# Attention and GEGLU block: the range flag's branch moved ahead of the last work, and a re-timed plan for the first chunks and the DMA transposes

## Chip, cores, metric

One core of one Trainium2 chip (eight cores; the others are unused). The metric is device time in microseconds of one execution, as the median of several runs. Engine names: PE is the matmul engine (TensorE), PEld its weight loads, ACT the scalar engine, DVE the vector engine, POOL GpSimd, SP the engine that issues most DMAs.

## What is computed

A pre-layernorm transformer block on 2048 tokens of width 512, bf16 inputs and output, with 32 heads of width 16 and an FFN width of 1792:

```python
x = A_x
h = x + attention(layernorm(x)) @ wo     # qkv = layernorm(x) @ wqkv; softmax(q k^T / 4) v, 32 heads
h2 = h + (gelu(n @ w_gate) * (n @ w_up)) @ w_down   # n = layernorm(h), tanh form of gelu
```

Most of the work is the softmax: 32 heads of 2048 x 2048 scores. A tile of the kernel is 128 keys by 512 query columns of one head (or of several heads with fewer queries each), so there are 2048 tiles, each of which needs 65,536 exponentials.

## The kernel before

**A fast program and a fallback.** `fast_path` computes the softmax without subtracting a row maximum. At its end `check` (L2031) compares all row sums with a safe range, reduces the comparison over partitions with one PE matmul and casts the sum to an integer `flag`, which is 128 if every row is in range. `max_path` is a second, complete program with a row maximum. In `emit` (L1183) each engine runs its fast instructions, waits until the flag is written, loads it into a register and branches: with 128 it jumps over its instructions of the fallback, otherwise it waits for the whole fast program and runs them. SP then waits for the final count of every DMA semaphore (L1194).

**A planned order.** The fast program is written as many generators ("streams") that yield operations with an engine, a planned duration, and the buffers that they read and write. The scheduler `Sched` (L889) plays them against each other: of the operations that are ready it takes the one that can start first, ties going to the stream with the lower priority number, to which a small random part (seed in L906) is added. What comes out is a fixed list per engine, with semaphore waits where a buffer is shared; the chip runs each list in order. So planned durations and priorities act only through the order. A planned DMA takes SP 0.5 us and lands after a time made of its size, a queue shared by all, and 0.8 us (L999 to L1003). `TTAB` is the planned time of an activation-table load; `PT` is a ring of 16 tiles, so ACT can be at most 16 tiles ahead of the products that consume them.

**Start.** `loads` (L1338) brings x in pieces (tiles 0 and 1, tiles 2 and 3, then four tiles at a time) and the weights, all on SP. For each tile of 128 tokens `ln1` (L1383) takes mean and variance on DVE, `ln1_rstd` (L1412) adds epsilon and raises to the power -0.5 on POOL, `ln1_norm` (L1420) normalizes, on DVE for tiles 0 to 7 and with three small-to-large POOL instructions for the others, and `ln1_T` (L1440) transposes: on PE with an evacuation by ACT (tiles 0 to 2) or DVE (3 to 7), by DMA for tiles 8 to 15. `first` (L1471) projects the keys and queries of the first 512 tokens; `proj_kq` and `proj_v` project the rest. `ones_v` (L1368) writes the ones beside V that make the row sums, with four POOL memsets once the first exponential is planned. Chunk 1 means tokens 512 to 1023 here (tiles 4 to 7); its streams have priority 9 (2 + 7c), the first chunk's -7 and below.

**Middle.** Score matmuls (L1582, recorded at L1329, the helper for matmuls in a part of the array) go to PSUM; ACT exponentiates two tiles in one instruction (L1335) into `PT`. A share of the tiles is exponentiated by DVE and POOL with integer arithmetic instead (`dget`, `dconv` L1706, `dchain` L1719 to L1726), from the 20th projection on. The products with V accumulate per unit; `ofin` (L1806) turns the result with a DMA transpose (OAT), divides, and per chunk of queries `leave` turns the heads' outputs (OT), `post` projects, adds x, normalizes and turns again (hT). Query chunks have 512, 512, 256, 256, 256, 128, 128 tokens. The FFN of a chunk (`gates`, `ups`, `downs`, L1943 to L2024) runs on PE beside the scores of later chunks. `fill` (L2054) puts dummy matmuls (L2052) where PE would idle.

**End.** After the last exponential only FFN work is left. `downs` (L2005) forms the down product of 128 tokens in one PSUM bank with 14 matmuls of 512 columns; `down_evac` (L2018) adds h on DVE and stores from SP. `check` has priority base_dl + 60, behind gates and ups (+30) and downs (+40).

## Time and profile before

| what | us |
|---|---|
| median of 5 runs | 818.82 (818.29 to 821.78) |
| the profiled execution | 820.27 |
| its span in the trace | 818.5 |
| PE busy | 793.9 (97%) |
| DVE busy | 759.2 (93%) |
| ACT busy | 766.7 (94%) |
| POOL busy | 251.9 (31%) |
| ACT exponentials (L1335), 776 of them | 722.4, mean 1.08 |
| DVE first step of its own tiles (L1706), 496 | 325.7, mean 0.68 |
| DMA transposes: OAT 31, OnT 15, hnT 15, xnT 8 | 2.3 to 2.4 from issue to landing (medians) |

The span is the time between the first and the last record of the profiled execution; the run's own time is 1.7 longer. Busy time of PE is modelled for overlapping matmuls, so a full PE need not be at its peak. A wait line names the waiting engine and line, then who released it, the total, the number and the longest. A timeline line has start, duration, engine, line, operation, output and input, count, and in brackets the idle time before it and who ended it. In the view by windows each engine's busy time in a stretch stands with its number of instructions, then the granted PE clock (1.00 is full). Register loads, branches and semaphore waits are not in these views, but the trace has records of them.

### The profile page before, as it was taken

Reading aid. Unit: us, or ns where it says so; the run is one execution under the profiler, and the core shown is the slowest. Engines: PE = TensorE matmul, PEld = TensorE weight load, DVE = VectorE, ACT = ScalarE, POOL = GpSimd, SP = SyncE. Lnnn points to the kernel's source line nnn. Section 1 sums busy time; section 2 is a strip of 40 time slices with the busy share of each in tenths; the row PEclk is TensorE's granted clock in tenths of the full one; section 3 lists DMA queues with packets and bytes.
Section 4 is the critical chain, followed back from the end, with each engine's and each line's share of the span. In section 5 each row is a group of like instructions: output and inputs, shape, how many; then the busy total and the mean of one; then the engine's idle time right before and its main releaser. Section 6 shows DMA issues by size and latency. Waiting matters only on the chain.

```text
span 818.5 us, 20339 instructions
## 1 busy us (share of the span) xinstructions
PE 793.9 (97%) x8325; PEld 277.9 (34%) x8325; DVE 759.2 (93%) x1238; ACT 766.7 (94%) x809; POOL 251.9 (31%) x305
## 2 busy tenths in 40 slices
PE   8999999999999999999999999999999999999997
PEld 3322222222222222222233333333343344444555
DVE  7569999999999999999989998999999999999974
ACT  4699999999999999999999999999999999999961
POOL 5714355423343221222243222223232231342220
PEclk9899999999999999999999999999999999999999
DMA  6200000700020000010021001000010200110000
GB/s 206 52 8 1 7 8 7 276 21 8 19 47 15 14 8 1 14 34 14 6 46 30 20 9 23 18 22 27 8 20 15 40 8 8 28 29 16 16 22 18
DMA packets 49878, 24.33 MB, mean 30 GB/s; under 512 B 39280, under 2 KB 48752, under 8 KB 49776
## 3 DMA queue, kind: packets, MB, share of 16 engines
q1 hardware_dynamic: 49776, 22.95, 11.0%
q8 instruction: 67, 1.10, 0.6%
q14 instruction: 35, 0.29, 0.1%
HBM read 11.80 MB, written 2.10 MB: 17 GB/s over the span
## 4 chain that ended last, share of the span: by engine, by line
PE 45%; DVE 31%; ACT 13%; issue 6%; DMA 3%; POOL 1%; SPq 0%; DVEq 0%; ACTq 0%; POOLq 0%
PE pbank L1329 27%; PE pbank L1328 16%; DVE dXE L1706 14%; ACT PT L1335 11%; DVE dXE L1721 6%; DVE dXE L1719 4%; DVE dXE L1726 4%; PE pbank L2052 1%; DVE GUT L1972 1%; DMA OAT<-OA 1%; ACT GUT L1985 1%; DMA wqkv_sb<-in_A_wqkv_dram 1%; DVE OA L1810 1%; POOL dXE L1723 1%; ACT L1335 1%
## 5 line engine op out<-in xcount | busy, mean ns | idle before, releaser
L1335 ACT ACTIVATE PT<-pbank 128x1024 bf16<-128x1024 f32 x776 | 722.4, 1082 | 17.5 <-PE pbank L1329 14.9
L1329 PE MATMUL pbank<-QT,KT 32*128 32x512 bf16 (+1 forms) x2304 | 346.4, 360 | 11.6 <-ACT PT L1335 3.6
L1706 DVE TENSOR_SCALAR dXE<-pbank 128x512 uint16<-128x512 f32 x496 | 325.7, 682 | 11.1 <-PE pbank L1329 9.7
L1723 POOL TENSOR_TENSOR dXE<-dXE 128x512 f16<-128x512 f16 x124 | 157.3, 1269 | 375.2 <-DVE dXE L1721 375.2
L1329 PEld LDWEIGHTS pbank<-QT,KT 32*128 32x128 bf16 x2304 | 89.2, 91 | 290.8 <-ACT PT L1335 201.1
L1329 PE MATMUL pbank<-PT,VA 128*32 128x256 bf16 (+2 forms) x2708 | 130.7, 293 | 0.0
L1721 DVE TENSOR_TENSOR dXE<-dXE 128x1536 f16<-128x1536 f16 x124 | 123.9, 1000 | 0.9
L1719 DVE TENSOR_SCALAR dXE<-dXE 128x2048 uint16<-128x2048 uint16 x124 | 92.4, 745 | 0.1
L1726 DVE TENSOR_SCALAR dXE<-dXE 128x2048 uint16<-128x2048 uint16 x124 | 87.9, 713 | 4.8 <-POOL dXE L1723 3.5
L1329 PE MATMUL pbank<-dXE,VA 128*32 128x256 f16 (+2 forms) x1752 | 76.6, 290 | 0.7 <-DVE dXE L1726 0.5
L1328 PE MATMUL pbank<-hnT_c,wg_sb 128*128 128x256 bf16 (+2 forms) x392 | 70.0, 291 | 0.3 <-issue 0.3
L1329 PEld LDWEIGHTS pbank<-PT,VA 128*32 128x32 bf16 x2708 | 48.2, 96 | 61.5 <-issue 58.6
L2052 PE MATMUL pbank<-ones_bf,zero_bf 128*128 128x512 bf16 x203 | 68.6, 388 | 0.0
L1328 PE MATMUL pbank<-hnT_c,wu_sb 128*128 128x256 bf16 (+2 forms) x392 | 59.3, 289 | 3.0 <-DVE GUT L2000 3.0
L1328 PE MATMUL pbank<-wd_sb,GUT 128*128 128x512 bf16 x224 | 60.1, 382 | 0.0
L1832 POOL TENSOR_TENSOR Otok<-OAT,LINV 128x128 bf16<-128x128 bf16 (+2 forms) x52 | 28.6, 564 | 82.6 <-DVE LINV L1826 82.5
L1329 PEld LDWEIGHTS pbank<-dXE,VA 128*32 128x32 bf16 x1752 | 30.9, 96 | 30.6 <-issue 17.4
L2000 DVE TENSOR_TENSOR GUT<-pbank,GUT 128x512 bf16<-128x512 f32 (+1 forms) x57 | 36.7, 673 | 2.5 <-ACT GUT L1985 1.5
L1328 PE MATMUL pbank<-xnT,wqkv_sb 128*128 128x512 bf16 (+1 forms) x152 | 38.4, 349 | 0.0
L1328 PEld LDWEIGHTS pbank<-hnT_c,wu_sb 128*128 128x128 bf16 x392 | 29.5, 98 | 25.0 <-issue 10.7
L1972 DVE CAST GUT<-pbank 128x512 bf16<-128x512 f32 (+1 forms) x53 | 35.6, 673 | 1.0 <-PE pbank L1328 0.7
L1328 PEld LDWEIGHTS pbank<-hnT_c,wg_sb 128*128 128x128 bf16 x392 | 24.7, 97 | 29.6 <-issue 27.1
(80 smaller groups left out, 348.6 us busy)
## 6 DMA issues: line engine op xcount, KB each, us to landing
xres<-in_A_x_dram SPq DMA_DIRECT2D x16, 128.0 KB, 2.3
out_dram<-out_sb SPq DMA_DIRECT2D x16, 128.0 KB, 1.7
wg_sb<-in_B_w_gate_dram SPq DMA_DIRECT2D x1, 1792.0 KB, 7.4
wu_sb<-in_B_w_up_dram SPq DMA_DIRECT2D x1, 1792.0 KB, 11.3
wd_sb<-in_B_w_down_dram SPq DMA_DIRECT2D x1, 1792.0 KB, 15.4
x_sb<-in_A_x_dram SPq DMA_DIRECT2D x3, 512.0 KB, 8.6
wqkv_sb<-in_A_wqkv_dram SPq DMA_DIRECT2D x1, 896.0 KB, 7.9
x_sb<-in_A_x_dram SPq DMA_DIRECT2D x2, 256.0 KB, 3.0
```

Of the source, the lines that this page charges most:

```text
L1328: return lambda e: e.matmul(o, l, r, start=start, stop=stop)
L1329: return lambda e: e.matmul(o, l, r, start=start, stop=stop, tile_position=tile)
L1335: return lambda e: e.activation(out=o, in_=i, func=func, **kw)
L1706: yield Op("dve", 0.603, lambda e: e.tensor_scalar(out=dXE[G["k"] % NX][:, 0, j, :], in0=pbank[:, b, :], scalar1=XMIN + 1024.0 * CENTER, s ...
L1719: yield Op("dve", 0.07 + 0.133 * n, lambda e: e.tensor_scalar(out=W, in0=X, scalar1=0x3ff, scalar2=0xb800, op0=ALU.bitwise_and, op1=ALU.bi ...
L1721: yield Op("dve", 0.066 + 0.267 * nd, lambda e: e.tensor_tensor(out=W[:, 0:nd, :].bitcast(F16), in0=W[:, 0:nd, :].bitcast(F16), in1=X[:, 0 ...
L1723: yield Op("pool", TPOOL, lambda e, j=j: e.tensor_tensor(out=W[:, j, :].bitcast(F16), in0=W[:, j, :].bitcast(F16), in1=X[:, j, :].bitcast( ...
L1726: yield Op("dve", 0.07 + 0.133 * (h1 - h0), lambda e, h0=h0, h1=h1: e.tensor_scalar(out=X[:, h0:h1, :], in0=X[:, h0:h1, :], scalar1=0x7c00 ...
L1832: yield Op("pool" if turned else "dve", 0.15 + 0.55 / len(slots) if turned else 0.06 + 0.28 / len(slots), lambda e, o4=o4, lx=lx, o_ap=o_a ...
L1972: yield Op("dve", 0.07 + 0.001042 * n * CHUNKS[c], lambda e: e.tensor_copy(out=o_ap, in_=i_ap), reads=[("pb", b)], writes=keys, extra=dE)
L2000: yield Op("dve", 0.07 + 0.001042 * n * CHUNKS[c], lambda e: e.tensor_tensor(out=o_ap, in0=u_ap, in1=o_ap, op=ALU.mult), reads=[("pb", b)] ...
L2052: return Op("pe", TMM, lambda e: e.matmul(pbank[:, b, :], zero_bf[:], ones_bf[:], start=False, stop=False, skip_group_check=True), reads=[ ...
```

## The change

- **Branch.** `Plan.run` can run a part of an engine's list. For ACT the list is cut in front of the last evacuations, for SP at the place where `check` has been planned; there the engine waits for the flag and branches. The rest of its list then stands in an `Else` (and, for the fallback, at the head of the `If`). PE, DVE and POOL branch at the end as before. SP's final waits are sorted by when the semaphore was last used.
- **Last token tile.** `last_down` makes two halves of 256 columns, in each of which an identity matmul puts h into PSUM first; `last_evac` copies each half out on ACT and stores it, one half from SP, the other from ACT.
- **Check.** Its priority becomes base_dl + 20.
- **DMA transposes.** SP is planned busy for 1.25 us, and the landing later by 2.0 us (OAT, OT, hT) or 0.6 (xT).
- **Start.** The ones are written by one DVE memset at priority -9; the memset of a PSUM bank comes ahead of the masks. Chunk 1's streams have priority -4 or -3.5, its key projection -5. Epsilon is added on DVE for tiles 4 to 7 too; DVE normalizes tiles 8 and 9 as well; POOL's two small factors become one instruction; ACT evacuates tiles 4 and 5. Planned load sizes differ.
- **Planner.** TTAB 1.3 becomes 1.45, the seed 9 becomes 66.

```diff
@@ Plan.dma
         self.dma_count[semkey] += 16
+        self.dma_last[semkey] = sum(self.dma_count.values())
...
-    def run(self, name, h):
+    def run(self, name, h, lo=0, hi=None):
         e = self.eng[name]
-        for (fn, waits, sig, dsem) in e.ops:
+        for (fn, waits, sig, dsem) in e.ops[lo:hi]:
...
@@ Sched
-        self.rng = random.Random(9)
+        self.rng = random.Random(66)
...
             self.done[tok] = self.pipe + 0.8
+            if op.dma[0] in TURNS:
+                self.t[op.eng] = start + 1.25
+                self.done[tok] += TURNS[op.dma[0]]
...
-TTAB = 1.3
+TTAB = 1.45
+TURNS = dict(OAT=2.0, OT=2.0, hT=2.0, xT=0.6)
...
@@ emit
-            P.run(name, h)
+            cut = P.cut.get(name, len(P.eng[name].ops))
+            P.run(name, h, 0, cut)
             h.wait_ge(P.sems["dve"], P.flag_count)
             r = h.alloc_register("flag_" + name)
             h.reg_load(r, flag[0:1, 0:1])
             with h.If_ne(r, 128):
+                P.run(name, h, cut)
                 for sem, v in fin:
                     if v:
                         h.wait_ge(sem, v)
                 FP.run(name, h)
+            if cut < len(P.eng[name].ops):
+                with h.Else():
+                    P.run(name, h, cut)
             if name == "sp":
-                for k, v in P.dma_count.items():
-                    h.wait_ge(P.sems[k], v)
+                for k in sorted(P.dma_count, key=lambda k: P.dma_last[k]):
+                    h.wait_ge(P.sems[k], P.dma_count[k])
...
@@ ones_v
-        for q in range(4):
-            yield Op("pool", 0.6, lambda e, q=q: e.memset(VA[:, 4 * q:4 * q + 4, :, 16:17], 1.0), writes=["VA_ones"], gate=lambda: C["exp"] >= 1, port=True)
-        yield Op("pool", 0.1, lambda e: e.memset(VF[:, NVA:NVA + 15], 0.0), writes=["VA_ones"])
+        yield Op("dve", 0.62, lambda e: e.memset(VA[:, :, :, 16:17], 1.0), writes=["VA_ones"])
+        yield Op("dve", 0.1, lambda e: e.memset(VF[:, NVA:NVA + 15], 0.0), writes=["VA_ones"])
...
@@ ln1, ln1_rstd, ln1_norm, ln1_T
-                if c == 0:
+                if c < 2:
...
-                sch.add(ln1_rstd(t), 2 + 7 * c if c else -7.5)
-            sch.add(ln1_norm(c, t), 2 + 7 * c if c else -7.5)
+                sch.add(ln1_rstd(t), (-4 if c == 1 else -7.5 if c == 0 else 2 + 7 * c))
+            sch.add(ln1_norm(c, t), (-4 if c == 1 else -7.5 if c == 0 else 2 + 7 * c))
...
-        if t >= 4:
+        if t >= 8:
...
-        if c < 2:
+        if t < 10:
...
-        if t in (0, 1, 2):
+        if t in (0, 1, 2, 4, 5):
...
@@ ofin
-            sch.add(check(), base_dl(c) + 60)
+            sch.add(check(), base_dl(c) + 20)
...
+    def last_down(c, qt):
+        q0 = g_at[c] + 128 * qt
+        for hf in range(2):
+            cs = slice(256 * hf, 256 * hf + 256)
+            b = yield Acquire(reads=["wd"], gate=lambda: C.get(("gut", c), 0) >= len(packs(c)) - 1)
+            yield Op("pe", 0.11, cols=256, fns=[MM(pbank[:, b, 0:256], ident[:], h_c[c][:, qt, cs], True, False)], reads=["ident", ("h", c, qt)], writes=[("pb", b)])
+            yield Wait(lambda: C.get(("gut", c), 0) == len(packs(c)))
+            for f0 in range(0, NFC, 7):
+                fcs = range(f0, f0 + 7)
+                yield Op("pe", 7 * 0.11, cols=256 * 7, fns=[MM(pbank[:, b, 0:256], GUT[:, fc, q0:q0 + 128], wd_sb[:, fc, cs], False, fc == NFC - 1) for fc in fcs],
+                         reads=["wd"] + [("GUT", fc, q0 // 128) for fc in fcs], writes=[("pb", b)])
+            sch.add(last_evac(c, qt, hf, cs, b), -20)
...
+    def last_evac(c, qt, hf, cs, b):
+        t = first_t[c] + qt
+        oi = t % 2
+        yield Wait(lambda: hasattr(P, "flag_count"))
+        yield Op("act", 0.28, lambda e: e.activation(out=out_sb[:, oi, cs], in_=pbank[:, b, 0:256], func=ACT.Copy), reads=[("pb", b)], writes=[("osb", oi) if hf == 0 else ("osb2", oi)],
+                 extra=lambda: P.cut.setdefault("act", len(P.eng["act"].ops)) and ())
+        sch.release(b)
+        yield Op("act" if hf else "sp", 0.06, lambda e: e.dma_start(out=outv[:, t, cs], in_=out_sb[:, oi, cs]), reads=[("osb", oi) if hf == 0 else ("osb2", oi)], writes=[("outd", t, hf)], dma=("outl", hf))
...
@@ check
         P.flag_count = P.eng["dve"].count
+        P.cut["sp"] = len(P.eng["sp"].ops)
```

## The prediction, before the result was known

> **What bounds the kernel now.** I first cut the span into stages with the view by windows: ScalarE's softmax exponentials (L1335) start at 14.5 and end at 789.
>
> ```profile
> core 0: us, PE busy (x) PEld busy (x) DVE busy (x) ACT busy (x) POOL busy (x), PEclk, DMA share, GB/s
> ...
> 14.50:22.70 8.20, 6.47 (x36) 1.82 (x35) 8.02 (x21) 6.63 (x7) 6.84 (x17) 0.85 0.07 22
> 22.70:30.20 7.50, 7.50 (x43) 3.26 (x42) 5.39 (x13) 1.03 (x2) 6.36 (x16) 0.70 0.30 67
> 30.20:38.00 7.80, 7.44 (x41) 1.93 (x40) 3.19 (x7) 7.43 (x8) 6.34 (x17) 1.00 0.24 54
> ...
> 60.00:789.00 729.00, 714.47 (x7666) 241.19 (x7667) 705.03 (x1115) 720.83 (x758) 223.84 (x234) 1.00 0.10 25
> 789.00:812.80 23.80, 23.78 (x335) 17.29 (x321) 13.73 (x30) 5.30 (x8) 0.79 (x2) 1.00 0.06 20
> 812.80:818.50 5.70, 0.00 (x0) 0.00 (x0) 0.69 (x1) 0.00 (x0) 0.00 (x0) 0.75 0.10 32
> ```
>
> Three regimes are to be seen. From 60 to 789 ACT (98.9%) and DVE (96.7%) share the exponentials and both are full; PE looks full, but the view by line counts 198 filler matmuls (L2052) there, at 0.217 each some 43 us that nobody needs. From 789 to 812.8 PE alone is full, with the rest of the FFN. Outside these the time is loose: 22.7 to 30.2, where ACT works 1.03 of 7.5, and the last 5.7, where almost nothing works. So I read those two ends in the timeline and the waits.
>
> Head, timeline and waits (us in total, times, longest):
>
> ```profile
> 14.34 2.75 POOL L1370 MEMSET VA<- 128x128 bf16 x4
> ...
> 17.53 0.57 POOL L1417 TENSOR_TENSOR rstd<-rstd,nhalf 128x1 f32<-128x1 f32 x1
> ...
> 18.13 0.73 DVE L1425 TENSOR_SCALAR xn_sb<-x_sb,mv,rstd 128x512 bf16<-128x512 bf16 x2
> ```
> ```profile
> 28.99 0.67 DVE L1514 CAST KT<-pbank 128x512 bf16<-128x512 f32 x1
> ...
> 30.20 7.44 ACT L1335 ACTIVATE PT<-pbank 128x1024 bf16<-128x1024 f32 x8 [6.10 <-PE pbank L1329]
> ```
> ```profile
> ACT PT L1335 <- PE pbank L1329: 9.1, 5, 6.1
> ```
>
> ACT's 6.1 us gap waits for scores, which wait for the keys of tokens 512 to 1023 (KT, 29.66). Back along that chain: tiles 5 and 6 are normalized only at 18.13, because POOL's rstd stood behind four memsets of VA; they are transposed at 22.97, evacuated from 23.61 to 25.82, with PE at half clock.
>
> Tail, timeline and the view of the output tensor:
>
> ```profile
> 812.81 0.69 DVE L2021 TENSOR_TENSOR out_sb<-pbank,h_c 128x512 bf16<-128x512 f32 x1 [2.44 <-PE pbank L1328]
> ```
> ```profile
> L2024 SPq DMA_DIRECT2D out_dram<-out_sb x2: 332/332/332, 808.3 to 813.5; - x2
> ...
> DMA to landing us min/median/max: 2.4/2.5/2.6
> ```
>
> The last store is issued at 813.53 and has landed by 816.2, yet the span ends at 818.53. The trace's sequencer records, which the views leave out, fill it: SP loads the flag at 813.92 (0.52), branches at 814.49 (0.06), and its next record is at 817.07; then 17 pairs of semaphore waits, 0.06 a pair, to 818.10, and 0.43 to the end. The landing is not what ends last; the branch is. After the same branch ACT is silent for 2.4 us (805.8 to 808.2), DVE 3.1, PE 3.4.
>
> **The tail, -2.6.** Removed from the path: everything behind SP's branch. Added, from E = 812.79, where PE finishes: the last token tile's down product becomes two halves of 256 columns, 2 x 14 matmuls at 0.108 for 14 at 0.216, which is even, plus two identity matmuls that add h. The first lies in front of the wait for the last products and is hidden, the second costs 0.11. The matmuls now come in sevens: the first seven need two products of L2000 where three needed one, and the last product ends at 810.37; I allow 0.2. E moves to 813.1. Then ACT evacuates 256 columns: Copy of that size took 0.47 (L1491), Gelu 0.39 (L1968); I take 0.47, the same function. The issue follows in 0.04. Landing: the 16 stores have a median of 1.7, the last two 2.4 to 2.6; in both of these, instruction fetches stood on the same engines, so I take 1.7. SP ends 0.5 later (last pair and close). 813.1 + 0.47 + 0.04 + 1.7 + 0.5 = 815.8, against 818.5: -2.7; I take -2.6 for the other queue. Bounds: -1.5 (landing 2.6, and ACT has issued no DMA in this trace, so a first-use cost of some tenths is open) to -2.9.
>
> [...] Queued behind ACT's wait are only the two evacuations and one store; behind SP's, the store of tile 14, ready at 808.25, and half of the last; nobody waits for that store. [...] DVE's and PE's own branches stay last: DVE's starts 2.4 us earlier, since its last add is gone, PE's ends near 814.7. Both are covered by the landing. The check's five DVE instructions already run at 799.9 to 801.9; nothing there.
>
> **The head, -4.0.** Chunk 1's normalization, key projection and rstd get priority; epsilon for tiles 4 to 7 moves to DVE; POOL loses the memsets (2.75), four epsilons (0.22 each), two normalizations (1.34 each with its factors) and one small op (0.21) on each of six tiles: 7.6 us. DVE gains one strided memset (some 0.7, while idle before 2.6), 4 x 0.1, two normalizations (0.33 each), and loses two copies of 0.33 to ACT. Chunk 1's x is there at 9.09; four tiles at about 1.2 on DVE and first-chunk evacuations (four of 0.35, two xnT of 0.3) give normalized tiles near 16, transposes and copies to 17, four matmuls (0.87) and evacuation to 19; allowing disorder, 21. ACT's first eight steps last until 22.5 at best, so the 6.1 gap can close.
>
> What is late next: PE. A stretch of eight steps (7.5 us of ACT) needs eight score pairs of 0.32, two PV groups of 0.54, four V tiles of 0.87 and one key projection of 0.87, 8.0 in all. So PE takes a part back: of ACT's 8.9 idle us from 14.5 to 46 I take 5.0 as recovered. An ACT us is not a us of span: ACT makes 2.14 tiles a us, while ACT and DVE together make (2 x 743 + 487) / 729 = 2.71. 5.0 x 2.14 / 2.71 = 4.0. Bounds: +0.9 (nothing closes and two xnT copies of 0.60 land between exponentials) to -7.0 (all 8.9).
>
> [...]
>
> **Transposes and the rest, -0.7.** The 69 DMA transposes run as before; the planner now counts 1.25 us of SP each and a landing later by 2.0 (0.6 for x). Real waits for them are 2.1 on DVE and 3.0 on PE:
>
> ```profile
> DVE LINV L1826 <- DMA OAT<-OA: 2.1, 3, 0.9
> ...
> PEld pbank L1328 <- DMA OnT<-Otok: 2.0, 3, 1.3
> ...
> PE pbank L1328 <- DMA OnT<-Otok: 1.0, 1, 1.0
> ```
>
> PE's lies in its slack; DVE's is 2.1 / 1.21 (DVE us a tile) / 2.71 = 0.6. TTAB, load sizes and the seed change only the order. The middle has 8.2 us of ACT idle and 24 of DVE idle for an order to win or lose in; the seed gets 0, +-3.
>
> Sum: -2.6 - 4.0 - 0.7 = -7.3. The profiled execution took 820.27 (span 818.53 and 1.74 around it), so 813.0 for such a one; the median of the runs is 818.82, so **811.5**.
>
> **Rivals.**
> A, tail only: PE or its half clock becomes the bound of the head and the gap moves instead of closing. For it: the 8.0 against 7.5 above. Against: the chain's first link, POOL, is really removed. 818.8 - 2.6 - 0.7 = 815.5. Chance 0.20.
> B, nothing gained: the end is set by a fetch that moved. A late flag puts ACT's load and branch (2.9) ahead of the last evacuation, and the head as in A. 818. [...] Chance 0.11.
> C, slower: FFN work slides behind the last exponential. Each chunk's chain has three transposes (OAT, OT, hT), planned 2 us later each, so about 6. Two chunks' chains make 12. PE work now ahead of 789 (chunk 4's gates 6.1, its ups 6.1, 9 of its 28 down matmuls 1.9, 32 of chunk 5's 56 gate matmuls 1.8) then falls into the PE-bound tail at full price. It decides from 9.8 us of slide (7.3 gained and 2.5); at 12 the time is 818.8 - 7.3 + 12 = 823.5. Against: PE idles or fills 58 us from 60 to 789, and the real landings don't change. Chance 0.08.
>
> **Numbers.** Forecast 0.61 (808 to 814.5). About 0.3%, 2.5 us, is what a measurement of this kernel tells from no change, so faster means under 816.4: the forecast and nearly all of A, 0.80; same 0.12; slower 0.08. The range must reach B: 806.5 to 818.0.
>
> **What would show it.** Tail: SP's and ACT's flag branches before 809, the last landing about 0.5 us ahead of the end, from PE's last matmul to the end 2.7 rather than 5.7. Head: KT of L1514 first near 20, no ACT wait of over 2 us before 46, no VA memset on POOL. Wrong if ACT idles 5 us or more between 14.5 and 46, if the PE-bound stretch behind the last exponential is much over 24, or if ACT's idle time from 60 on exceeds 11.

## The result, and the profile after

| | before | changed |
|---|---|---|
| median us | 818.82 | 814.61 (814.12 to 822.0) |
| ratio of the two | 1 | 0.9943 (0.9931 to 0.9955) |
| the profiled execution: own time / span | 820.27 / 818.5 | 815.01 / 813.2 |
| last exponential ends (X) | 789.2 | 787.1 |
| PE's last matmul ends (E) | 812.8 | 810.5 |
| from E to the end | 5.75 | 2.75 |
| granted PE clock, median run | 0.996 | 1.00 |
| ACT idle, first exponential to 46 / 46 to X | 8.8 / 8.2 | 4.7 / 8.5 |
| exponential instructions of ACT / tiles of DVE | 776 / 496 | 778 / 492 |
| DVE's last own tile ends | 778.5 | 774.2 |

The kernel became 4.2 us faster in the medians (0.51%; the ratio, 0.57%), where 7.3 were forecast. The profiled execution of before lies 1.5 above its median and that of the changed kernel 0.4 above, so a difference of two spans (5.3) shows about one us too much. I keep to the medians for sums and use the spans for places. The row on the clock comes from the list of runs, in which each has its own mean granted clock; it turns out to matter, and the experiments come back to it.

Lines of the changed kernel have moved: L1335 is now L1347, L1329 L1341, L1328 L1340, L1706's record L1715. The view by windows of the changed kernel, in the stages of before:

```profile
core 0: us, PE busy (x) PEld busy (x) DVE busy (x) ACT busy (x) POOL busy (x), PEclk, DMA share, GB/s
14.50:22.70 8.20, 7.25 (x48) 2.50 (x46) 7.89 (x23) 7.23 (x9) 3.93 (x10) 1.00 0.08 27
22.70:30.20 7.50, 7.17 (x48) 2.02 (x49) 6.29 (x15) 6.74 (x8) 6.25 (x13) 1.00 0.39 87
30.20:38.00 7.80, 7.77 (x50) 1.93 (x48) 3.09 (x5) 6.95 (x8) 3.65 (x8) 1.00 0.43 52
38.00:46.00 8.00, 6.84 (x42) 2.00 (x46) 3.16 (x5) 5.91 (x7) 0.00 (x0) 1.00 0.00 0
60.00:789.00 729.00, 715.63 (x7704) 239.97 (x7703) 702.64 (x1105) 720.04 (x756) 224.42 (x233) 1.00 0.10 25
```

In the second row ACT works 6.74 of 7.5 where it worked 1.03, and the granted clock is 1.00 where it was 0.85 and 0.70. In the last, ACT is as full as before (98.8%) and DVE a little less (96.4%).

The hole at 24 to 30 in the timeline of the changed kernel:

```profile
16.43 0.55 POOL L1428 TENSOR_TENSOR rstd<-rstd,nhalf 128x1 f32<-128x1 f32 x1 [0.63 <-DVE rstd L1419]
...
17.46 0.41 DVE L1436 TENSOR_SCALAR xn_sb<-x_sb,mv,rstd 128x512 bf16<-128x512 bf16 x1
...
22.30 0.68 DVE L1523 CAST KT<-pbank 128x512 bf16<-128x512 f32 x1
...
23.46 7.45 ACT L1347 ACTIVATE PT<-pbank 128x1024 bf16<-128x1024 f32 x8 [1.73 <-PE pbank L1341]
...
31.76 7.56 ACT L1347 ACTIVATE PT<-pbank 128x1024 bf16<-128x1024 f32 x8 [0.84 <-PE pbank L1341]
```

The keys of tokens 512 to 1023 are evacuated at 22.30, where it was 28.99, and the 6.10 us in front of ACT's next stretch are 1.73. The gap is nearly closed. What is left comes later: ACT waits 2.08 us in front of its stretch that starts at 41.41, and the chain of waits names the reason:

```profile
33.72 0.10 issue
33.81 0.78 POOL xn_sb L1442
34.59 0.02 issue
34.60 4.31 DMA xnT<-xn_sb
38.91 0.25 issue
39.16 1.89 PE pbank L1340 x8
41.04 0.33 PE pbank L1341 x4
```

POOL still normalizes the last six tiles one after the other (the last at 33.81), then come a DMA transpose and two key projections on PE.

The end in the timeline of the changed kernel:

```profile
799.74 0.14 DVE L2079 CAST flag<-pbank 1x1 int32<-1x1 f32 x1 [0.71 <-PE pbank L2078]
...
808.86 0.39 ACT L2034 ACTIVATE out_sb<-pbank 128x256 bf16<-128x256 f32 x1 [7.36 <-PE pbank L1340]
809.27 0.33 SPq L2037 DMA_DIRECT2D out_dram<-out_sb  x1
810.50 0.39 ACT L2034 ACTIVATE out_sb<-pbank 128x256 bf16<-128x256 f32 x1 [1.25 <-PE pbank L1340]
810.91 0.37 ACTq L2037 DMA_DIRECT2D out_dram<-out_sb  x1
```

The flag is there 9 us ahead of ACT's first evacuation, so ACT's branch lies inside the 7.36 us in which ACT has nothing to do. The trace's sequencer records around it, times in us:

| record | before | changed | branch at the end (late_branch, below) |
|---|---|---|---|
| SP loads the flag / branches | 813.92 / 814.49 | 799.91 / 800.43 | 809.32 / 809.88 |
| ACT branches / its next record | 805.8 / 808.2 | 801.57 / 803.99 | 811.49 / 813.98 |
| SP's pairs of waits, first to last | 817.07 to 818.10 | 809.66 to 812.78 | 812.70 to 813.80 |
| last landing | 816.2 | 812.73 | 812.93 |
| PE's own branch ends | 814.36 | 812.86 | 812.66 |
| end of span | 818.53 | 813.2 | 814.3 |

In the changed kernel SP has gone through 16 of its 18 pairs by 810.62, while the last stores are still in flight; the last two pairs come with the landings, 0.02 us behind each. That is the order which the prediction wanted.

### The profile page after: what moved, and what is told of

It is laid out like the page before. It is cut to its first block, busy times and chain, and to the rows that moved or that the text cites. A ratio compares the mean times of both kernels' runs of the same rounds, so it can differ in the third digit from the quotient of the medians.

```text
span 813.2 us, 20343 instructions
## 1 busy us (share of the span) xinstructions
PE 792.3 (97%) x8342; PEld 275.9 (34%) x8342; DVE 759.2 (93%) x1236; ACT 770.4 (95%) x815; POOL 246.5 (30%) x283
## 4 chain that ended last, share of the span: by engine, by line
PE 51%; DVE 28%; ACT 10%; issue 5%; POOL 2%; DMA 1%; DVEq 0%; ACTq 0%; POOLq 0%
PE pbank L1341 32%; PE pbank L1340 15%; DVE dXE L1715 12%; ACT PT L1347 8%; DVE dXE L1730 5%; DVE dXE L1728 4%; PE pbank L2090 4%; DVE dXE L1735 4%; DVE GUT L1981 1%; ACT GUT L1994 1%; POOL dXE L1732 1%; DVE OA L1819 1%; DMA xnT<-xn_sb 1%; ACT L1347 0%; POOL xn_sb L1442 0%
## 5 line engine op out<-in xcount | busy, mean ns | idle before, releaser
L1347 ACT ACTIVATE PT<-pbank 128x1024 bf16<-128x1024 f32 x778 | 724.6, 1086 | 13.5 <-PE pbank L1341 10.5
L1341 PE MATMUL pbank<-QT,KT 32*128 32x512 bf16 (+1 forms) x2304 | 346.9, 359 | 8.4 <-DVE dXE L1715 3.3
L1715 DVE TENSOR_SCALAR dXE<-pbank 128x512 uint16<-128x512 f32 x492 | 323.8, 682 | 8.8 <-PE pbank L1341 6.7
L1732 POOL TENSOR_TENSOR dXE<-dXE 128x512 f16<-128x512 f16 x123 | 155.3, 1263 | 369.4 <-DVE dXE L1730 369.4
L1341 PEld LDWEIGHTS pbank<-QT,KT 32*128 32x128 bf16 x2304 | 89.2, 91 | 294.6 <-ACT PT L1347 202.6
L1341 PE MATMUL pbank<-PT,VA 128*32 128x256 bf16 (+2 forms) x2708 | 130.1, 292 | 0.0
L1728 DVE TENSOR_SCALAR dXE<-dXE 128x2048 uint16<-128x2048 uint16 x123 | 94.6, 769 | 0.1
L1735 DVE TENSOR_SCALAR dXE<-dXE 128x2048 uint16<-128x2048 uint16 x123 | 88.3, 721 | 5.8 <-POOL dXE L1732 4.7
L1341 PE MATMUL pbank<-dXE,VA 128*32 128x256 f16 (+2 forms) x1752 | 76.2, 289 | 2.0 <-DVE dXE L1735 1.9
L1340 PE MATMUL pbank<-hnT_c,wg_sb 128*128 128x256 bf16 (+2 forms) x392 | 70.4, 291 | 0.0
L1341 PEld LDWEIGHTS pbank<-PT,VA 128*32 128x32 bf16 x2708 | 47.4, 96 | 60.4 <-issue 57.2
L2090 PE MATMUL pbank<-ones_bf,zero_bf 128*128 128x512 bf16 x201 | 66.0, 386 | 0.0
L1340 PE MATMUL pbank<-hnT_c,wu_sb 128*128 128x256 bf16 (+2 forms) x392 | 58.0, 289 | 3.9 <-DVE GUT L2009 3.2
L1340 PE MATMUL pbank<-wd_sb,GUT 128*128 128x512 bf16 (+1 forms) x238 | 59.9, 369 | 0.0
L1341 PEld LDWEIGHTS pbank<-dXE,VA 128*32 128x32 bf16 x1752 | 31.0, 96 | 32.2 <-issue 17.0
L1340 PE MATMUL pbank<-xnT,wqkv_sb 128*128 128x512 bf16 (+1 forms) x152 | 38.2, 349 | 1.3 <-DMA xnT<-xn_sb 1.2
L1340 PEld LDWEIGHTS pbank<-hnT_c,wu_sb 128*128 128x128 bf16 x392 | 29.7, 98 | 24.1 <-issue 9.1
L1533 POOL TENSOR_SCALAR QT<-QT,qmask 128x512 bf16<-128x512 bf16 x30 | 26.3, 883 | 33.0 <-DVE QT L1530 32.2
## 6 DMA issues: line engine op xcount, KB each, us to landing
wd_sb<-in_B_w_down_dram SPq DMA_DIRECT2D x1, 1792.0 KB, 15.3
```

Of the source, the lines that this page charges most:

```text
L1340: return lambda e: e.matmul(o, l, r, start=start, stop=stop)
L1341: return lambda e: e.matmul(o, l, r, start=start, stop=stop, tile_position=tile)
L1347: return lambda e: e.activation(out=o, in_=i, func=func, **kw)
L1715: yield Op("dve", 0.603, lambda e: e.tensor_scalar(out=dXE[G["k"] % NX][:, 0, j, :], in0=pbank[:, b, :], scalar1=XMIN + 1024.0 * CENTER, s ...
L1728: yield Op("dve", 0.07 + 0.133 * n, lambda e: e.tensor_scalar(out=W, in0=X, scalar1=0x3ff, scalar2=0xb800, op0=ALU.bitwise_and, op1=ALU.bi ...
L1732: yield Op("pool", TPOOL, lambda e, j=j: e.tensor_tensor(out=W[:, j, :].bitcast(F16), in0=W[:, j, :].bitcast(F16), in1=X[:, j, :].bitcast( ...
```

## Experiments

To place a gain, I counted from the traces how many of the 2048 tiles ACT and DVE had exponentiated by a given time:

| by us | before | tail_only | changed | head_only | no_turns | seed0 |
|---|---|---|---|---|---|---|
| 60 | 85 | 90 | 99 | 91 | 93 | 99 |
| 100 | 197 | 201 | 209 | 203 | 202 | 207 |
| 300 | 765 | 770 | 779 | 759 | 768 | 783 |
| 500 | 1300 | 1300 | 1296 | 1291 | 1306 | 1320 |
| 750 | 1959 | 1963 | 1968 | 1939 | 1950 | 1967 |

The first two kernels have the same start, yet differ by some 4 tiles (1.5 us at 2.71 a us); part of this is the PE clock, which was at half for 6.8 us from 20.3 in before's profile and for 3.4 us from 20.9 in tail_only's. Ratios below are to the kernel before, run beside each.

**tail_only: the end alone.** Before, with the hunks of the branch, the last token tile and the check; start, planned times and seed are the old ones.

```diff
+            cut = P.cut.get(name, len(P.eng[name].ops))
+            P.run(name, h, 0, cut)
...
-            sch.add(check(), base_dl(c) + 60)
+            sch.add(check(), base_dl(c) + 20)
...
+            if c == NC - 1 and qt == CHUNKS[c] // 128 - 1:
+                yield from last_down(c, qt)
```

> The kernel before with the last token tile in two halves, the branches of ACT and SP ahead of the last work, and the check's better priority; head, transposes' planned times and seed as before. Theory (three parts that add: tail, head, re-dealt middle): the last exponential ends at 789.2 as before, from PE's last matmul to the end 2.7 us rather than 5.7, the time 2.9 below before, 815.9. Rival (the tail gains only together with the new head, since the flag comes early only there): 817.5 or more.

Measured 815.95, ratio 0.9964 (0.9947 to 0.998), 2.9 under before. From E to the end it takes 3.06 where it took 5.75. So the end is worth what was forecast, alone too, and all the rest of the change brings 1.3 (815.95 to 814.61). The flag did not need the new start to come early, as the rival had it. In its profile X is 787.1, not the 789.2 that was expected; before's profile was a long execution.

The end holds in the other profiles too. Of the runs below with the new end and the early branch, all but one take 2.8 to 3.6 us from E to the end; seed0 took 5.9 (see the section on the hardware). The two below with the old end, head_only and plan_only, take 5.7 and 5.9.

**head_only: the start alone.** Before, with the new start only; old planned times and seed.

```diff
-        if c < 2:
+        if t < 10:
...
-        if t in (0, 1, 2):
+        if t in (0, 1, 2, 4, 5):
...
-    sch.add(ones_v(), 5)
+    sch.add(ones_v(), -9)
```

> The kernel before with the changes of the start alone (chunk 1's priority, ones on DVE, POOL's smaller share, planned load sizes). Theory (the head's lead is given back by the re-dealt middle of the changed kernel): 12 tiles or more ahead of before at 100 us, and 4.0 to 4.5 less at the end, 814.5. Rival (a lead in the head cannot last, because DVE's share shrinks as it is consumed): the same lead at 100, but only about 2 less at the end, 816.7.

Measured 833.46, ratio 1.017 (1.0146 to 1.0193): 14.6 us slower, a miss of everything expected. Its waits from 46 to 800 (DVE, then ACT; total, times, longest):

```profile
DVE dXE L1703 <- PE pbank L1329: 12.9, 35, 1.4
DVE LINV L1823 <- DMA OAT<-OA: 6.4, 7, 1.5
DVE GUT L1997 <- PE pbank L1328: 6.0, 7, 3.3
```
```profile
ACT PT L1335 <- PE pbank L1329: 12.7, 24, 3.2
```

The loss does not stand in the start: ACT idles 6.7 to 46, less than before, and the count is 6 tiles ahead at 100 (12 were expected). By 300 it is 6 behind. So the loss lies in the middle, whose order was dealt anew: both engines wait for scores, and DVE three times as long for transposes as before (6.4 for 2.1). Two things besides the order's waits are on record. Seed 9 was a good one for the kernel before (its planned end is the second lowest of 150 seeds) and is not for this one (the 107th), and the granted clock of the five runs is 0.985 to 0.991, where a typical run of before has 0.996. Both come back below.

**plan_only: the planned times and the seed alone.**

```diff
+            if op.dma[0] in TURNS:
+                self.t[op.eng] = start + 1.25
+                self.done[tok] += TURNS[op.dma[0]]
...
-TTAB = 1.3
+TTAB = 1.45
...
-        self.rng = random.Random(9)
+        self.rng = random.Random(66)
```

> The kernel before with only the planner's numbers changed: transposes' planned times, table load 1.45, seed 66. Theory (the middle's new order costs): about 2 more than before, 821, with the exponentials ending at 791. Rival (the order is neutral): 818.8, within 0.8.

Measured 822.69, ratio 1.004 (1.0016 to 1.0064): 3.8 slower, the theory's direction and nearly twice its size; X is 794.4 where 791 was expected. DVE does 480 tiles of its own instead of 496, ACT 784 exponential instructions instead of 776. So neither part is a gain by itself: 14.6 and 3.8 us lost, yet with the end they make a kernel 4.2 faster. The parts don't add; each deals a new order of the whole middle, with a seed that was not chosen for it (seed 66 is the second lowest of 150 planned ends for the changed kernel, the 102nd for this one).

**late_branch: the changed kernel with its branch at the end of the lists.** The halves of the last tile stay.

```diff
-            cut = P.cut.get(name, len(P.eng[name].ops))
+            cut = len(P.eng[name].ops)
```

> The changed kernel with the flag's branch at the end of ACT's and SP's work again; the last token tile stays in two halves, evacuated by ACT and stored from both. Theory (a branch costs about 0.6 for load and branch and 2.5 to the next instruction, SP's begins 1.2 before PE's end because the first half is stored early): SP's waits start at 812.8 and end at 813.9, ACT's fetch ends at 814.3, the end at 814.4 to 814.9, so 1.2 to 1.7 more than the changed kernel. Rival (the whole 3 us of the tail is the branch): 3 more.

Measured 816.12, ratio 0.9959 (0.9946 to 0.9972), 1.5 slower than the changed kernel, as expected. The table above shows where: SP's first wait comes only at 812.70, after its own branch, and 18 pairs follow. So 1.5 of the 2.9 us is the place of the branch (from E to the end it takes 4.16, for 2.75); the other 1.4 comes with the halves, the second queue, the earlier check and the order of SP's waits, which weren't taken apart.

**seed9 and no_turns: what made head_only lose?** One theory (S) was the seed: the old seed is a bad one for the new start. The other (D) was the planned times: with the new start, an order made with transposes that are planned too short doesn't hold on the chip. seed9 is the changed kernel with the old seed; no_turns has the new seed and the old planned times.

```diff
-        self.rng = random.Random(66)
+        self.rng = random.Random(9)
```

> The changed kernel with seed 9, the seed of before. The start alone, with seed 9 and the old transposes' times, took 833.5, 19 more than the changed kernel after 3 for the tail is allowed for 16. Theory S (the order is a lottery, and seed 66 a good ticket for this head): near 828, with DVE's exponential tiles well under 490 and 28 us or more behind the last exponential. Theory D (the transposes' longer planned times repair the order, since DVE no longer stands before a DMA that hasn't landed): 815 to 817, DVE's waits for OAT under 1 us.

Measured 818.62, ratio 1.0004 (0.9991 to 1.0016): 4.0 slower than the changed kernel: between the two theories, and much nearer D's 815 to 817 than S's 828. DVE has no wait for OAT among its listed ones, as D said, and does 484 tiles, as S said.

```diff
-            if op.dma[0] in TURNS:
+            if False:
...
-TTAB = 1.45
+TTAB = 1.3
```

> The changed kernel with the transposes and the table load planned as before (seed 66 kept). Theory D (planned times repair the order): 822 or more, DVE waits 5 us or more for OAT. Theory S (the seed matters, not the times): 813 to 817.

Measured 825.59, ratio 1.0087 (1.0061 to 1.0113): 11.0 slower than the changed kernel, which is D's side. Waits of DVE from 46 to 790, in no_turns:

```profile
DVE dXE L1715 <- PE pbank L1341: 14.0, 23, 1.2
...
DVE LINV L1835 <- DMA OAT<-OA: 3.0, 4, 1.1
```

And from 46 to 783 in the changed kernel:

```profile
DVE dXE L1715 <- PE pbank L1341: 6.7, 19, 1.3
DVE dXE L1735 <- POOL dXE L1732: 4.7, 6, 1.3
```

There the wait for OAT is gone altogether. But only 3.0 us of DVE's waiting in no_turns stand at a transpose, where D expected 5 or more; most of the rest is waiting for scores. D has the time right, and its direct wait explains only a small part of it. That the 11.0 is not seed 66's luck alone is seen at seed 9, where the same exchange of planned times is worth 11.9 (head_only to seed9 is 14.8, of which the end is 2.9). Not all of this need be the waits: the granted clock differs as well (below).

**seed1 and seed0: two more orders of the changed kernel.**

```diff
-        self.rng = random.Random(66)
+        self.rng = random.Random(1)
```

> The changed kernel with seed 1: a second ticket. Theory S: anywhere from 815 to 830, unlike seed 66 by 3 or more. Theory D: within 2 of the changed kernel, 813 to 817.

Measured 816.71, ratio 0.9984 (0.9971 to 0.9998), 2.1 from the changed kernel: inside D's range, and S had left room for it too.

```diff
-        self.rng = random.Random(66)
+        self.rng = random.Random(0)
```

> The changed kernel with seed 0. The plan's own end (its last planned time, which knows nothing of the chip's surprises) is 804.7, against 805.9 for seed 66, 809.8 for seed 1 and 814.3 for seed 9, which ran in 814.6, 816.7 and 818.6. Theory S (seeds with the same start differ by what the rest of the order makes of the lead): 813.4 to 814.6, at or a little below the changed kernel, with 493 or more DVE tiles. Rival (seed 66 was the lucky end of the lottery on the chip and a planned end says nothing): 816 or more.

Measured 812.93 (810.57 to 816.52), ratio 0.9913 (0.9887 to 0.994): the fastest version, 6.0 under before, though its interval overlaps that of the changed kernel a little. It has 488 DVE tiles where the theory asked for 493 or more, so the count of DVE's tiles does not rank these orders. Four seeds with the same start, end and planned times thus give 812.9, 814.6, 816.7 and 818.6: a spread of 5.7 us, above what the whole start was forecast to bring.

**ones_pool: the ones back on POOL.**

```diff
-        yield Op("dve", 0.62, lambda e: e.memset(VA[:, :, :, 16:17], 1.0), writes=["VA_ones"])
+        for q in range(4):
+            yield Op("pool", 0.6, lambda e, q=q: e.memset(VA[:, 4 * q:4 * q + 4, :, 16:17], 1.0), writes=["VA_ones"], gate=lambda: C["exp"] >= 1, port=True)
...
-    sch.add(ones_v(), -9)
+    sch.add(ones_v(), 5)
```

> The changed kernel with the ones beside V written by POOL's four memsets again, after the first exponential is planned. Theory (POOL's memsets were the first link of the head's gap): keys of tokens 512 to 1023 2 to 3 us later than 22.98 and ACT idle from 14.5 to 46 by 2 or more above the changed kernel's 4.7; the whole time +1.5 to +2.5 unless the order is dealt anew, which can add several us either way. Rival (the priority of chunk 1 alone closes the gap): keys by 23.5, idle within 1 of 4.7.

Measured 819.33, ratio 1.0008 (0.9996 to 1.0019), 4.7 slower. The keys of tokens 512 to 1023 are there at 25.86 instead of 22.98, which is the theory's 2 to 3 us, so the memsets do hold up that chain. But ACT idles 5.1 to 46 instead of 4.7, as the rival had it, and X is 787.7 instead of 787.1. The time went behind X, where 27.2 us of FFN are left instead of 23.4. That is another order again, so of the memsets' own cost in the whole time the run says only that it is small where the rest of the new start is there.

**old_start and norm_dve: what the start is worth.** old_start has the new end and planned times with the old start, at a seed whose plan was good (120). norm_dve is the changed kernel with two of POOL's six normalizations on DVE (seed 129), against the gap at 39 to 41.

```diff
-        yield Op("dve", 0.62, lambda e: e.memset(VA[:, :, :, 16:17], 1.0), writes=["VA_ones"])
+        for q in range(4):
+            yield Op("pool", 0.6, lambda e, q=q: e.memset(VA[:, 4 * q:4 * q + 4, :, 16:17], 1.0), writes=["VA_ones"], gate=lambda: C["exp"] >= 1, port=True)
...
-        if t < 10:
+        if c < 2:
```

> The changed kernel with the start of before (chunk 1 at its low priority, ones and factors on POOL, old planned load sizes) and seed 120, whose planned end, 807.6, is the lowest of 150 seeds for this combination; the new start's is 804.7 to 805.9. It is the worth of the start with a chosen order on both sides. Theory (the start's lead of 12 tiles is worth 4.4 us, and a good order keeps it): 818 to 819. Rival (most of the lead is given back whatever the order, because PE and DVE have the same work left): 815.5 to 816.5, 1 to 2 above the changed kernel.

Measured 816.29, ratio 0.9969 (0.9952 to 0.9986). ACT idles 6.4 to 46. The old start costs 1.7 against the changed kernel, which is the rival's side (1 to 2), and 3.4 against seed0. It is one order against two; over 150 seeds each, the planner's own median end is 1.6 us later with the old start (1.3 with the old planned times), far from the 4.0 of the forecast.

Its head bears on how much of ACT's gap belonged to the clock. In the first two stages of the views by windows, old_start never falls to half clock:

```profile
core 0: us, PE busy (x) PEld busy (x) DVE busy (x) ACT busy (x) POOL busy (x), PEclk, DMA share, GB/s
14.50:22.70 8.20, 7.31 (x51) 2.51 (x49) 8.13 (x21) 6.12 (x8) 6.66 (x16) 1.00 0.04 14
22.70:30.20 7.50, 7.31 (x45) 2.37 (x43) 7.07 (x16) 4.63 (x7) 6.35 (x16) 1.00 0.30 69
```

| start | profile | us at half clock from 14 to 46 | longest ACT wait | ACT idle to 46 | tiles by 60 / 100 |
|---|---|---|---|---|---|
| old | before | 6.8 | 6.1 | 8.8 | 85 / 197 |
| old | plan_only | 6.8 | 4.7 | 8.7 | 85 / 196 |
| old | tail_only | 3.4 | 5.0 | 7.7 | 90 / 201 |
| old | old_start | 0 | 2.9 | 6.4 | 98 / 206 |
| new | changed | 0 | 2.1 | 4.7 | 99 / 209 |

Of the changed kernel's lead of 12 tiles at 100 us, an old start at full clock has 9. This doesn't give all 9 to the clock: old_start's order also normalizes tile 5 at 15.24, ahead of the wait for POOL, where before does so at 18.13, and the two weren't separated. But against an old start in a good order and at full clock the new one is only 3 tiles ahead, 1.1 us.

The edit of norm_dve, beside its seed:

```diff
-        if t < 10:
+        if t < 10 or t >= 14:
```

> The changed kernel with tiles 14 and 15 normalized by DVE too, which is idle 60% there, and seed 129 (planned end 804.6). Theory (the last gap of the head, 2.1 us at 41, waits for POOL's chain of 2.2 us a tile): ACT idle from 14.5 to 46 falls from 4.7 to about 2.7, 2 to 4 tiles more at 100 us, time 812.5 to 814. Rival (PE's projections hold the scores at 41 anyway): idle within 0.7 of 4.7.

Measured 813.21, ratio 0.993 (0.9903 to 0.9957). ACT idles 4.6 to 46, as in the changed kernel and as the rival said, so what remains of the gap did not close, and that it is 1.4 faster is within the seeds' spread.

**old_times: seed 0 with the old planned times.**

```diff
-            if op.dma[0] in TURNS:
-                self.t[op.eng] = start + 1.25
-                self.done[tok] += TURNS[op.dma[0]]
...
-TTAB = 1.45
+TTAB = 1.3
```

> The changed kernel with transposes and table load planned as before, and seed 0, the lowest planned end of 150 seeds for that (805.0). Theory D (with the old times the plan promises what the chip doesn't keep: planned end to measured was 15 for seed 66 with the old times, 4 to 9 with the new): 816 to 820. Theory S (only the seed matters): 813.5 to 815.

Measured 816.75, ratio 0.9978 (0.9956 to 0.9999), 3.8 slower than seed0, as theory D expected, but a third of the loss at seeds 9 and 66.

The runs side by side, with two more numbers. The planned end is the end time that the planner itself gave that order, which the kernel's program computes as it is built. The clock column is the median of the runs' granted clocks, and in brackets the time times what it lacks to 1, in us: an estimate of what PE would lose to it if PE had work throughout (in before's head the matmuls of L1448 follow each other every 0.107 us at half clock and every 0.056 at full clock). It is an upper bound, for a stretch in which PE has no matmul counts in it too: in before's profile the clock is at half again from 815.6, and PE's last matmul ends at 812.8.

| kernel | planned times | median | planned end | median minus planned, less 2.9 for an old end | clock (us) |
|---|---|---|---|---|---|
| before | old | 818.8 | 805.1 | 10.8 | 0.996 (3.3) |
| tail_only | old | 815.95 | 805.0 | 10.9 | 0.998 (1.6) |
| old_times | old | 816.75 | 805.0 | 11.8 | 0.996 (3.3) |
| no_turns | old | 825.6 | 810.3 | 15.3 | 0.994 (5.0) |
| head_only | old | 833.5 | 810.1 | 20.5 | 0.989 (9.2) |
| changed | new | 814.6 | 805.9 | 8.7 | 1.000 (0) |
| seed0 | new | 812.9 | 804.7 | 8.2 | 0.998 (2.0) |
| seed1 | new | 816.7 | 809.8 | 6.9 | 0.999 (0.8) |
| seed9 | new | 818.6 | 814.3 | 4.3 | 1.000 (0) |
| ones_pool | new | 819.3 | 815.0 | 4.4 | 1.000 (0) |
| norm_dve | new | 813.2 | 804.6 | 8.6 | 1.000 (0) |
| old_start | new | 816.3 | 807.6 | 8.6 | 1.000 (0) |
| plan_only | new | 822.7 | 813.4 | 6.4 | 0.997 (2.5) |

The column before the last falls into two groups that don't overlap: with the old planned times the chip takes 10.8 to 20.5 us longer than the plan, with the new ones 4.3 to 8.7. The groups' means lie 6.8 apart. It would be natural to call this an order that the chip keeps better, but two other things can account for most of it. A plan with longer transposes is itself longer: over 150 seeds its median end is 1.6 to 1.9 later. And the clocks differ: the bracketed losses average 4.5 with the old times and 0.7 with the new. Taken off, the groups are 7.5 to 11.3 and 3.9 to 8.7: they overlap, 3.0 apart in the mean, of which the longer plan is 1.6 to 1.9. So 1.1 to 1.4 us of the 6.8 are left for orders that are kept better (an estimate from these columns; it is more where less of the bracket was really lost). Within the new group the planned end ranks the orders nearly as the chip does.

**Time goes with the clock in one and the same kernel.** Of the changed kernel's 28 runs whose clock is listed, 27 at 1.00 took 814.1 to 815.5, and the one at 0.989 took 822.0. old_times took from 814.9 (0.998) to 823.25 (0.985). Of the 88 runs of before that were made beside the experiments, the six at 0.999 or more have a median of 817.3, the six at 0.992 or less 823.3. Before at nearly full clock thus lies 2.7 above the changed kernel at full clock, which is what the end is worth; the other 1.5 of the 4.2 go with the clock. tail_only's one run at 1.00 took 815.04, 0.4 above the changed kernel. For head_only, 5.9 of the 14.6 us can be clock (9.2 less before's 3.3), and the planner itself foresaw 5.0; for no_turns up to 5.0 and 4.4 of its 11.0. Whether in a given run the clock fell first or a stall of PE, these lists don't tell; nor does any run show what made it fall in these orders, and whether the planned times had a part in it.

## Why the prediction was right or wrong

**The tail, -2.6: right, in size and mechanism.** tail_only measured -2.9. Term by term in the changed kernel's trace: evacuation 0.39 (0.47 taken) and 0.02 to the issue, landing 1.82 from the issue's start (1.7), close 0.47 (0.5). That is 2.70, against 2.75 from E to the end. ACT's first DMA issue, for which some tenths were left open, took 0.37 beside SP's 0.33 here, and 1.81 in seed0's profile (last section). The flag came at 799.74, 5.4 earlier than before (805.15), and ACT's first record behind its branch (803.99) stands 4.9 ahead of its first evacuation (808.86). The length of the branch record is not what decides: on ACT it is 0.04 and the next record follows 2.4 later, and moving the branch alone was worth 1.5 us, more than SP's load and branch records in before take together (0.52 and 0.06). What the prediction had too loose is the cover: PE's own branch was to end at 814.7, 0.6 ahead of the last landing (815.3) and 1.1 ahead of the end. It ends at 812.86, 0.13 behind the last landing (812.73), and PE's last record ends level with SP's. So a shorter landing alone would probably gain little before PE's branch moves too; no run tried it.

**The head, -4.0: the gap closed, its worth was mis-sized.** Idle time recovered to 46 is 4.1, where 5.0 was taken, and the first exponential starts 1.2 earlier, which was not counted; the first key projection came at 22.3 rather than near 20. Some durations were not those of the traces: a normalization on DVE took 0.39 and a copy of xnT 0.42 (0.33 taken), an evacuation of the first chunk 0.42 to 0.47 (0.35), the memset of the ones 0.49 (0.7). The changed head ran at full clock, with PE busy 88% of 14.5 to 22.7 (7.25 of 8.20), where before's had a clock of 0.85 with 79% (6.47). old_start is at full clock there too, with PE 89% busy, so the half clock was not a property of the old start; what made it fall in before's execution, no run shows.

That is the first thing the term had wrong. The gap of 6.1 us, and with it the 5.0, was read from an execution with 6.8 us of half clock, and all of it was put down to the start. The half clock stood in the forecast as a risk to the new head (rival A), not as a part of the old gap. At full clock and in another order the old start leaves a longest wait of 2.9 (old_start), and the new one is 3 tiles ahead of it, 1.1 us, not 4.0.

The second is the step from there to the end. At 100 us the count was 12 tiles ahead of before, 8 ahead of tail_only: 3.0 to 4.4 us. The step "5.0 x 2.14 / 2.71 = 4.0" matched these two profiles up to there. It failed in carrying this lead on to X unchanged. X is only 2.1 earlier than in before's profile, and no earlier than tail_only's (787.1 in both). Where the lead went is read from ACT's sum up to X: 1.2 from an earlier first exponential and 4.1 from idle time; against it two exponentials more (724.6 busy for 722.4), two copies of xnT more (1.2, named in the bounds and left out of the sum) and 0.3 more idle later. That makes 5.3 - 3.7 = 1.6 of the 2.1. The group of DVE's own tiles has the other side of it:

```profile
L1715 DVE TENSOR_SCALAR dXE<-pbank 128x512 uint16<-128x512 f32 x492 | 323.8, 682 | 8.8 <-PE pbank L1341 6.7
```

The new order gives DVE 492 tiles where it had 496, and DVE is done with them at 774.2, 4.3 us earlier than before and 12.9 ahead of X (10.7 before). What DVE was spared, ACT did. This is the account of this one order against before's, not a rule: seed0, the fastest, has 488 DVE tiles, and old_start, slower by 3.4, has 496.

**Transposes and the seed, -0.7: too small a matter made of the order.** The direct wait (0.6, the 0.7 was rounded up) went, as taken. But exchanging the planned times was worth 11 us at seed 66, 11.9 at seed 9 and 3.8 at seed 0 with the new start, and nothing with the old one between tail_only (815.95) and old_start (816.29), which have a good seed each. "The seed gets 0, +-3" had about the right width (four seeds span 5.7), yet it was booked as a side term of the transposes, when order and clock together move the time by more than the whole head was forecast to bring. The clock of the whole execution was not a term of the sum at all.

In all: -2.9 for the end as forecast, -1.3 for start and planned times together where -4.7 was, and as far as one run of tail_only at full clock tells, 0.9 of this 1.3 goes with the clock. The time came out 3.1 above the forecast, just outside its own span of 808 to 814.5, and 0.9 under rival A's 815.5. A's reason is not what happened, however: the gap didn't move to PE in the head, it closed, and what that is worth was small. Rival B's late flag and rival C's slide didn't happen either: the stretch from X to E is 23.4 where it was 23.6. Of the signs of success two failed: the keys came at 22.3, and ACT had one wait of over 2 us before 46 (2.08). None of the signs that were named for a wrong forecast came, for none of them looked at what happens to the lead between 46 and X.

**Open.** Which of the three planned times (SP's occupation, the landing, the table load) matters wasn't separated. That orders made with them are kept better is shown for seeds 9 and 66 with the new start, and there mixed with the clock; for orders with a good planned end it is small (11 against 8 to 9 us over the plan, before the clock and the longer plan are taken off). That lost time goes through waits for transposes is shown only for 3 to 6 us of DVE's waiting. Why some orders run at a lower clock stays open. How much of any one order's time is luck can't be told from one seed each.

## What to carry to other kernels

Where a planner deals the whole order, a local edit is not simply worth its local gain; compare several orders of both versions, with a seed chosen for each, before pricing it. Look at the granted clock of every run first: a gap read from an execution at half clock may not be the edit's to close, and a difference between two versions may be the clock's if one of them ran at a lower one. An edit at the very end, behind all shared work, has no such second effect and can be summed from the trace (here 2.6 forecast, 2.9 measured). Giving the planner the latencies that the trace shows helped at three seeds with this start and not with the other.

## What the runs showed of the hardware

- A store of 128 x 256 has 16 parts, and one of them can be late: in the changed kernel SP's half had 15 parts landed by 810.81 and the last at 812.51, while PE's branch record was running. In seed0's profile the last store's issue on ACT took 1.81 us instead of 0.37, and one part landed 2.0 after the others:

```profile
808.14 0.68 ACT L2034 ACTIVATE out_sb<-pbank 128x256 bf16<-128x256 f32 x2 [3.04 <-PE pbank L1340]
...
808.55 0.33 SPq L2037 DMA_DIRECT2D out_dram<-out_sb  x1
808.85 1.81 ACTq L2037 DMA_DIRECT2D out_dram<-out_sb  x1
```

  From E to the end it took 5.9 there, as much as before the change. So the gain of the tail rests on a landing that can be some 3 us later. This profile was the longest of seed0's six runs (816.52).
- PE's record of its far branch lasts 3.4 to 4.1 us (before 810.97 to 814.36, changed 808.91 to 812.86, late_branch 808.57 to 812.66), while on ACT and SP the record takes 0.04 to 0.06 and the next instruction comes 2.4 to 2.8 us later. In the traces of before and of the changed kernel a transfer of 8 or 16 KB on an instruction queue starts 0.9 to 1.1 us behind the start of each engine's branch (before: ACT 805.81 and 806.73, PE 810.97 and 811.91, SP 814.49 and 815.44; changed: ACT 801.57 and 802.48, PE 808.91 and 809.85). The trace doesn't say for which engine a transfer is.
- The granted clock fell to half in stretches of 3.4 or 6.8 us, also far from the start and the end: at 267.8 and 776.4 in head_only, 318.1 in old_times, 501.1 in seed0, 711.1 in seed1, 805.7 in no_turns. The same kernel has executions with and without: the changed kernel's run at 0.989 took some 7.4 us longer than its others.
